# Layout of the inverse DFT's output and of the gated result, between PSUM, VectorE and the last projection

## The chip, the core and the metric

The kernel runs on one core of a Trainium2 chip. The metric is the device time of one execution in microseconds. Inside the core, TensorE multiplies matrices from SBUF into PSUM (PE is the multiplication, PEld the load of the stationary operand, the "weights"), VectorE (DVE) and ScalarE (ACT) work on vectors and read PSUM, GpSimd (POOL) works on SBUF, and SyncE (SP) issues DMA transfers.

## The reference

Two blocks follow each other, on four sequences of 6272 steps with 256 channels, all in float32.

```python
sig = 1 / (1 + exp(-f_logit)); f = lower_bound + (1 - lower_bound) * sig; i = 1 - f
h = f[:, t] * h + i[:, t] * x[:, t]          # for each t; x = all h
proj = x @ w_proj                            # 256 -> 3 * 256: x1, x2, x3
X2 = rfft(x2, axis=1); H = rfft(filter_fft, axis=0)
x2_conv = irfft(X2 * H, n=6272, axis=1)      # a circular convolution over the sequence
out = (x1 * x2_conv * x3) @ w_out
```

## The kernel before

Time is written as 128 x 49: a step t has an index m (128) and a residue r (49). The Fourier transform over 6272 is done as a transform over m, one over r, the product with the filter's transform, and the two inverses, all as matmuls. float16 is used for most operands; the last projection takes float32r, a four-byte matmul type.

The stages for a batch b are these.

- `hgrn(b)`: x and f_logit are loaded in 13 chunks of up to 512 steps (L275), the sigmoid runs on ScalarE (L278), the product on GpSimd (L280), both are turned with channels on the partitions (L287), the recurrence is a scan on VectorE (L304), x1 and x3 are projected (L315) and multiplied into z (L323, L326). z[b] keeps x1 * x3 in float16, channels on the partitions and time along the free axis.
- `wraps`, `phase_p`, `phase_f1`, `mini`: copies of h, the x2 projection (L589), the transform over m (L604).
- `units(b)`: 16 units with the transform over r (L648), the product with the filter (L658) and the inverse over r (L668), whose result is left in Th.
- `phase_o(b)`: the output. It runs over r in twelve groups of four and a last group of one (rn is the size of the group). For each group it does the inverse DFT over m into two banks of PSUM, one for each half p of the channels (L693, two 64-row matmuls for each r and p), the gate: the product with z into the buffer ys (L700), the projection with w_out, in which ys is the stationary operand (L710, two matmuls for each r, 256 columns each), the copy out of PSUM into one of two output buffers (L715, in helper lines L248 on ScalarE and L253 on VectorE), and the store (L719). ys has two buffers, taken in turn; PSUM has eight banks, and L693 and L710 each take two at a time.

In the kernel before, a group's PSUM bank and its ys row hold the time index m outside and the residue i inside: element m * rn + i. Thus L693 writes every rn-th element of the bank, the gate reads and writes one run, and L710's weights `y[:, kh, :, i]` are every rn-th element of the row. z is read as `zr[:, :, :, r0:r0 + rn]`, runs of rn elements with a step of 49 between runs.

The order of the work isn't that of the program text. `op` records each piece with a cost for each engine that may do it, its reads and its writes; `Plan.emit` then issues the pieces by a list scheduler that uses these costs and an estimate of transfer times. So hgrn(b + 1) is interleaved with units(b) and phase_o(b) on every engine, and each engine then carries out its own list in that order. The first `emit` covers the preparation of the filter and hgrn(0), the second all the rest.

The preparation has similar shapes: L519 is a float32r matmul of 256 columns whose weights are contiguous, the copy behind it reads PSUM with the residue innermost, 256 elements apart, in a helper line (L251 on VectorE, into f), and L379 writes weights with a step of four float16 elements.

Of the kernel before, what the change touches and what calls it, by code (L numbers as in the profile page):

```python
# [46 lines left out]
def m0_of(r):  # L47
    return (128 * q_of(r) - r) // Q


class Plan:
# [20 lines left out]
    def op(self, cost, fn, r=(), w=(), kb=0.0, table=None, take=0, src=None):  # L72
        preds = set()
        for t in r:
            if t in self.writer:
                preds.add(self.writer[t])
        for t in w:
            if t in self.writer:
                preds.add(self.writer[t])
            preds.update(self.readers.get(t, ()))  # L80
        me = len(self.ops)
        if src is not None:
            preds.add(src)
            self.ops[src]["users"].append(me)
        self.ops.append(dict(cost=cost, fn=fn, preds=preds, kb=kb, table=table, end=None,
                             eng=None, succ=[], take=take, src=src, users=[], at=None))
        for p in preds:
            self.ops[p]["succ"].append(me)
        for t in r:
            self.readers.setdefault(t, set()).add(me)  # L90
        for t in w:
            self.writer[t] = me
            self.readers[t] = set()
        return me
# [89 lines left out]
def kernel(  # L184
# [10 lines left out]
    nc = tc.nc  # L195
# [36 lines left out]
    PS = psp.tile([128, 8, 512], F32, name="PS")  # L232
# [10 lines left out]
    def copy(e, dst, src, scale=None):  # L243
        if e == "ACT":
            if scale is None:
                nc.scalar.copy(dst, src)  # L246
            else:
                nc.scalar.activation(dst, src, AF.Copy, scale=scale)  # L248
        elif e == "DVE":
            if scale is None:  # L250
                nc.vector.tensor_copy(dst, src)  # L251
            else:
                nc.vector.tensor_scalar(dst, in0=src, scalar1=scale, scalar2=None,  # L253
                                        op0=AOP.mult)
        else:
            nc.gpsimd.tensor_copy(dst, src)

    def either(n, runs=1.0):

        return {"ACT": 0.06 + runs * n / 1200.0, "DVE": 0.08 + runs * n / 960.0}  # L260
# [418 lines left out]
    def phase_o(b):  # L679
        zr = zt[b % 2][:].rearrange("p k (m r) -> p k m r", r=Q)  # L680
        tf = Th[:].rearrange("p c a g -> p (c a g)")
        for g, r0 in enumerate(range(0, Q, 4)):
            rn = min(4, Q - r0)

            def inv(e, cb, r0=r0, rn=rn):
                for i in range(rn):
                    r = r0 + i
                    sh = (128 - m0_of(r)) % 128
                    for rr in range(2):
                        c0 = (rr * Q + r) * 128  # L690
                        for p in range(2):
                            ps = slice(64 * p, 64 * p + 64)
                            nc.tensor.matmul(PS[:, cb + p, i:i + rn * 127 + 1:rn],  # L693
                                             tf[ps, c0:c0 + 128], ID[ps, rr, sh:sh + 128],
                                             start=(rr == 0), stop=(rr == 1))
            i1 = op({"PE": 0.235 * rn}, inv, r=[("Th", u) for u in range(NU)] + ["Th"], take=2)
            yk = g % 2
            y = ys[:, yk, :, 0:rn * 128].rearrange("p a (m i) -> p a m i", i=rn)
            op({"DVE": 0.08 + rn * 0.27}, lambda e, cb, y=y, r0=r0, rn=rn:
               nc.vector.tensor_tensor(  # L700
                   y, PS[:, cb:cb + 2, 0:rn * 128].rearrange("p a (m i) -> p a m i", i=rn),
                   zr[:, :, :, r0:r0 + rn], op=AOP.mult),
               r=[("z", b % 2, jb, c) for jb in range(2) for c in range(NCHK)],
               w=[("y", yk)], src=i1)

            def proj(e, ob, y=y, rn=rn):
                po = PS[:, ob:ob + 2].rearrange("m a (r e) -> m (a r) e", e=256)
                for i in range(rn):
                    for kh in range(2):
                        nc.tensor.matmul(po[:, i, :], y[:, kh, :, i], Wo[:, kh, :],  # L710
                                         start=(kh == 0), stop=(kh == 1))
            po = op({"PE": 0.34 * rn}, proj, r=[("y", yk)], take=2)
            k = count["o"] % 2
            count["o"] += 1
            op(either(256 * rn), lambda e, ob, k=k, rn=rn: copy(  # L715
                e, osb[k][:, 0:rn, :],
                PS[:, ob:ob + 2].rearrange("m a (r e) -> m (a r) e", e=256)[:, 0:rn, :], OS),
               r=[("x2o", i) for i in range(14)] if k else [], w=[("osb", k)], src=po)
            op({"SP": 0.5}, lambda e, k=k, r0=r0, rn=rn: nc.sync.dma_start(  # L719
                out[b].rearrange("(a r) d -> a r d", r=Q)[:, r0:r0 + rn, :],  # L720
                osb[k][:, 0:rn, :]),
               r=[("osb", k)] + ([("x2o", i) for i in range(14)] if k else []), kb=128 * rn)
# [8 lines left out]
    with tc.manual_schedule():  # L731
# [13 lines left out]
        ys = cv.tile([128, 2, 2, 512], F32R, name="ys")  # L745
# [7 lines left out]
        for b in range(B):  # L753
            units(b)
            phase_o(b)
            if b + 1 < B:
                hgrn(b + 1)
                wraps()
                phase_p(b + 1)
                phase_f1(b + 1)  # L760
                mini(b + 1)
# [31 lines left out]
```

## Time and profile before

| What | Value |
|---|---|
| Time, median of 3 runs | 654.3 us (652.3 to 658.98) |
| The profiled execution: time, and the span from its first to its last instruction | 655.55 us, 653.4 us |
| Mean granted TensorE clock in it | 0.953 |
| PE, DVE, ACT, POOL busy | 86%, 78%, 58%, 23% of the span |
| DMA, mean rate | 199 GB/s |

The profile lists busy time by engine, the chain of work that ended last (followed back from the last instruction, at each step to what released it), and groups of instructions: line, engine, operation, output and inputs by name, shape, count, then busy time and mean duration in ns, then the idle time before them with what ended it. A line of a windows view gives a stretch of the span, its length, the busy time of each engine (with the count of instructions), the granted clock, the busy share of the DMA engines and what they moved. A timeline row gives start, duration and count of merged instructions. The row of a single line gives minimum, median and maximum duration. Names are cut by the program: X, for instance, stands for X2, and the second output buffer lies in X2.

### The profile page before, as it was taken

The page shows a single profiled execution, that of the slowest core. Times are in us where ns is not written, and L with a number is a line of the kernel's source. Part 1 is how long each engine was busy: PE and PEld are TensorE (multiplying, and loading weights), DVE is VectorE, ACT ScalarE, POOL GpSimd, SP SyncE. Part 2 cuts the span into 40 slices and gives each one's busy share as a digit, 9 for nine tenths or more (in the row PEclk, how much of TensorE's full clock was granted, in tenths as well). Part 3 has the DMA queues.
Part 4 walks back from the last instruction along what each step waited for, and adds up shares of the span by engine and source line. Part 5 has one row for each costly group of instructions (what it writes and reads, how often), then busy time and mean ns, then how long its engine had stood idle before and what let it go on. Part 6 is the DMA issues. An engine that isn't in the chain of part 4 may idle for free.

```text
span 653.4 us, 12392 instructions
## 1 busy us (share of the span) xinstructions
PE 559.9 (86%) x4821; PEld 430.0 (66%) x4821; DVE 512.2 (78%) x576; ACT 381.2 (58%) x490; POOL 149.8 (23%) x161
## 2 busy tenths in 40 slices
PE   3677888977799999897769999988789999968997
PEld 3455555764478886774538986954568887644786
DVE  7768787589978769699889467899987668999632
ACT  3788786794343558793445456964456567833333
POOL 5424420122104223213222132031023220011000
PEclk9989999899979999998898999999899999997898
DMA  8957755556659786435698588134598862055144
GB/s 310 382 178 256 237 164 172 178 170 192 179 167 333 245 300 211 146 129 180 196 266 266 180 276 282 65 97 148 159 258 293 301 219 108 1 162 160 41 186 170
DMA packets 77643, 130.09 MB, mean 199 GB/s; under 512 B 4878, under 2 KB 56146, under 8 KB 77586
## 3 DMA queue, kind: packets, MB, share of 16 engines
q1 hardware_dynamic: 77586, 129.31, 59.9%
q8 instruction: 38, 0.62, 0.4%
q14 instruction: 19, 0.16, 0.1%
HBM read 84.54 MB, written 32.11 MB: 179 GB/s over the span
## 4 chain that ended last, share of the span: by engine, by line
PE 53%; DVE 14%; DMA 13%; ACT 7%; issue 5%; POOL 2%; SPq 1%; DVEq 0%; ACTq 0%; POOLq 0%
PE PS L710 13%; PE PS L287 10%; PE PS L315 8%; DVE PP L658 8%; PE PS L693 6%; DMA FL<-in_f_logit_dram 6%; PE PS L589 5%; PE PS L668 3%; PE PS L604 2%; PE PS L648 2%; DVE HA L304 2%; ACT X L246 2%; DMA XT<-in_x_dram 2%; DMA H<-HA 2%; DMA Hu<-H 2%
## 5 line engine op out<-in xcount | busy, mean ns | idle before, releaser
L280 POOL TENSOR_TENSOR XT<-XT,FL 128x1024 f32<-128x1024 f32 (+1 forms) x52 | 116.4, 2238 | 266.4 <-DMA XT<-in_x_dram 117.6
L658 DVE TENSOR_TENSOR PP<-PS,Hu 98x1008 f16<-98x1008 f32 x128 | 145.6, 1200 | 8.9 <-PE PS L648 3.0
L246 ACT CAST X<-PS 128x784 f16<-128x784 f32 (+2 forms) x92 | 91.7, 1007 | 84.4 <-PE PS L668 77.2
L304 DVE TENSOR_TENSOR_SCAN HA<-fTs,HA,PS 128x512 f16<-128x512 f32 (+1 forms) x96 | 114.6, 1205 | 29.2 <-PE PS L287 20.7
L315 PE MATMUL PS<-HA,W 128*128 128x512 f16 (+1 forms) x416 | 106.5, 376 | 6.0 <-DVE HA L304 3.9
L299 ACT ACTIVATE fTs<-PS,nomc 128x512 f32<-128x512 f32 (+1 forms) x104 | 69.5, 669 | 65.2 <-PE PS L287 46.1
L710 PE MATMUL PS<-Wo,ys 128*128 128x256 f32 x392 | 102.5, 405 | 0.5 <-DVE ys L700 0.5
L710 PEld LDWEIGHTS PS<-Wo,ys 128*128 128x128 f32 x392 | 94.1, 325 | 5.6 <-issue 3.7
L700 DVE TENSOR_TENSOR ys<-PS,z 128x1024 fp32r<-128x1024 f32 (+1 forms) x52 | 60.6, 1178 | 42.0 <-PE PS L693 37.6
L668 PEld LDWEIGHTS <-PP 98*128 98x128 f16 x1024 | 55.8, 105 | 51.4 <-POOL PP L651 20.9
L668 PE MATMUL PS<-VA,PP 98*128 98x98 f16 x512 | 62.7, 220 | 21.7 <-DVE PP L658 9.9
L323 ACT ACTIVATE x1s<-PS 128x512 f32<-128x512 f32 (+1 forms) x104 | 59.0, 576 | 33.1 <-PE PS L315 23.7
L326 DVE TENSOR_TENSOR z<-PS,x1s 128x512 f16<-128x512 f32 (+1 forms) x104 | 66.4, 651 | 14.9 <-ACT x1s L323 10.4
L287 PE MATMUL PS<-iden,FL 128*128 128x128 f32 x392 | 67.1, 296 | 12.4 <-ACT FL L278 12.4
L287 PE MATMUL PS<-iden,XT 128*128 128x128 f32 x392 | 65.3, 289 | 8.9 <-POOL XT L280 7.3
L278 ACT ACTIVATE FL<-FL 128x1024 f32<-128x1024 f32 (+1 forms) x52 | 52.5, 1010 | 22.2 <-DMA FL<-in_f_logit_dram 22.1
L287 PEld LDWEIGHTS PS<-iden,XT 128*128 128x128 f32 x392 | 48.1, 148 | 25.2 <-POOL XT L280 10.4
L315 PEld LDWEIGHTS <-W 128*128 128x128 f16 x416 | 37.4, 100 | 39.3 <-issue 15.3
L668 PE MATMUL PS<-VB,PP 98*128 98x98 f16 x512 | 62.5, 220 | 0.0
L287 PEld LDWEIGHTS PS<-iden,FL 128*128 128x128 f32 x392 | 49.3, 152 | 19.6 <-ACT FL L278 9.8
L648 PE MATMUL PS<-HA,FT 64*128 64x512 f16 x256 | 41.8, 402 | 20.8 <-ACT X L246 19.2
L693 PE MATMUL PS<-ID,X 64*128 64x128 f16 x784 | 51.3, 309 | 1.0 <-ACT X L248 0.5
(90 smaller groups left out, 583.4 us busy)
## 6 DMA issues: line engine op xcount, KB each, us to landing
Hu<-H SPq DMA_DIRECT2D x64, 392.0 KB
FL<-in_f_logit_dram SPq DMA_DIRECT2D x48, 512.0 KB
XT<-in_x_dram SPq DMA_DIRECT2D x48, 512.0 KB
out_dram<-X SPq DMA_DIRECT2D x24, 512.0 KB
out_dram<-osb SPq DMA_DIRECT2D x24, 512.0 KB
HA<-in_moe_filter_fft_dram SPq DMA_DIRECT2D x12, 512.0 KB
HA<-HA SPq DMA_DIRECT2D x16, 384.0 KB
H<-HA SPq DMA_DIRECT2D x16, 196.0 KB
```

The lines of the kernel that those rows point to most:

```text
L246: nc.scalar.copy(dst, src)
L280: op({"POOL": 0.1 + 0.535 * nb}, lambda e, xt=xt, ft=ft: nc.gpsimd.tensor_tensor(xt, xt, ft, op=AOP.mult), r=[("ft", k)], w=[("xt", k)])
L287: nc.tensor.transpose(PS[:, p, j * 128:(j + 1) * 128], src[:, j, cols], iden[:])
L299: nc.scalar.activation(fT, PS[:, p, 0:n], AF.Identity, scale=nomc[:, kh:kh + 1], bias=1.0),
L304: nc.vector.tensor_tensor_scan(h, fT, PS[:, p, 0:n], init, op0=AOP.mult, op1=AOP.add),
L315: nc.tensor.matmul(PS[:, p, 0:n], W13[:, kh, js], HA[:, HB[kh] + t0:HB[kh] + t0 + n], start=(kh == 0), stop=(kh == 1))
L326: nc.vector.tensor_tensor(zz, PS[:, p, 0:n], xs, op=AOP.mult),
L658: nc.vector.tensor_tensor(PP[:TB, k, o, :, :, 1:64], px.unsqueeze(1).broadcast_to([TB, 2, UE, 63]), hh[:, :, :, 1:64], op=AOP.mult)
L668: nc.tensor.matmul(PS[:, ib + o, pr * TB:(pr + 1) * TB], PP[:TB, k, o, n, 2 * pr:2 * pr + 2, :], v[:TB], start=(n == 0), stop=(n == 1))
L693: nc.tensor.matmul(PS[:, cb + p, i:i + rn * 127 + 1:rn], tf[ps, c0:c0 + 128], ID[ps, rr, sh:sh + 128], start=(rr == 0), stop=(rr == 1))
L700: nc.vector.tensor_tensor(y, PS[:, cb:cb + 2, 0:rn * 128].rearrange("p a (m i) -> p a m i", i=rn), zr[:, :, :, r0:r0 + rn], op=AOP.mult),
L710: nc.tensor.matmul(po[:, i, :], y[:, kh, :, i], Wo[:, kh, :], start=(kh == 0), stop=(kh == 1))
```

## The change

The inverse DFT over m is written as 128 consecutive elements for each r: element i * 128 + m. The gate keeps its order of iteration (m outside, i inside), so it now reads PSUM and writes ys with a step of 128 four-byte elements between neighbours, and reads z as before. `y` keeps its form for the projection, so each L710 load takes 128 consecutive elements of ys. In the group with rn = 1 nothing differs. The costs that the planner is given are not changed.

```diff
@@ phase_o
-                            nc.tensor.matmul(PS[:, cb + p, i:i + rn * 127 + 1:rn],
+                            nc.tensor.matmul(PS[:, cb + p, i * 128:(i + 1) * 128],
                                              tf[ps, c0:c0 + 128], ID[ps, rr, sh:sh + 128],
                                              start=(rr == 0), stop=(rr == 1))
             i1 = op({"PE": 0.235 * rn}, inv, r=[("Th", u) for u in range(NU)] + ["Th"], take=2)
             yk = g % 2
-            y = ys[:, yk, :, 0:rn * 128].rearrange("p a (m i) -> p a m i", i=rn)
+            y = ys[:, yk, :, 0:rn * 128].rearrange("p a (i m) -> p a m i", i=rn)
             op({"DVE": 0.08 + rn * 0.27}, lambda e, cb, y=y, r0=r0, rn=rn:
                nc.vector.tensor_tensor(
-                   y, PS[:, cb:cb + 2, 0:rn * 128].rearrange("p a (m i) -> p a m i", i=rn),
+                   y, PS[:, cb:cb + 2, 0:rn * 128].rearrange("p a (i m) -> p a m i", i=rn),
                    zr[:, :, :, r0:r0 + rn], op=AOP.mult),
```

## The prediction

> **What bounds the kernel now.** I read the page first: busy shares, then the chain that ended last.
>
> ```profile
> span 653.4 us, 12392 instructions
> ...
> PE 559.9 (86%) x4821; PEld 430.0 (66%) x4821; DVE 512.2 (78%) x576; ACT 381.2 (58%) x490; POOL 149.8 (23%) x161
> ...
> PE 53%; DVE 14%; DMA 13%; ACT 7%; issue 5%; POOL 2%; SPq 1%; DVEq 0%; ACTq 0%; POOLq 0%
> PE PS L710 13%; PE PS L287 10%; PE PS L315 8%; DVE PP L658 8%; PE PS L693 6%; DMA FL<-in_f_logit_dram 6%; PE PS L589 5%; PE PS L668 3%; PE PS L604 2%; PE PS L648 2%; DVE HA L304 2%; ACT X L246 2%; DMA XT<-in_x_dram 2%; DMA H<-HA 2%; DMA Hu<-H 2%
> ```
>
> TensorE holds half of the chain; the two lines whose operands change, L693 and L710, hold 19% of the span. But VectorE is 78% busy, and the change gives it work. So I cut the span into stretches: the first four below are the four output phases (the first three with the next batch's recurrence interleaved), the last four the unit phases.
>
> ```profile
> core 0: us, PE busy (x) PEld busy (x) DVE busy (x) ACT busy (x) POOL busy (x), PEclk, DMA share, GB/s
> 186.00:252.00 66.00, 65.13 (x500) 55.19 (x500) 50.35 (x49) 35.05 (x49) 19.25 (x10) 0.98 0.80 268
> 357.00:400.00 43.00, 42.02 (x326) 36.46 (x322) 25.43 (x25) 21.74 (x29) 9.87 (x6) 1.00 0.74 253
> 487.00:542.00 55.00, 53.71 (x414) 45.89 (x413) 36.60 (x37) 34.21 (x47) 17.64 (x10) 1.00 0.79 275
> 610.00:650.00 40.00, 37.65 (x300) 33.25 (x297) 16.50 (x16) 13.01 (x16) 0.00 (x0) 0.99 0.36 145
> 121.00:186.00 65.00, 49.52 (x583) 37.10 (x581) 58.97 (x55) 37.97 (x41) 13.72 (x21) 0.97 0.61 181
> 293.00:357.00 64.00, 48.43 (x477) 35.31 (x478) 56.29 (x52) 28.63 (x38) 18.08 (x22) 0.87 0.74 222
> 431.00:487.00 56.00, 45.72 (x471) 29.09 (x470) 55.01 (x58) 26.24 (x38) 9.78 (x18) 0.97 0.56 165
> 570.00:610.00 40.00, 31.25 (x329) 18.50 (x328) 38.06 (x37) 14.56 (x19) 5.05 (x16) 0.83 0.43 132
> ```
>
> In the first three (A, B, C) PE is full (65.13 of 66, 42.02 of 43, 53.71 of 55) while DVE has 15.7, 17.6 and 18.4 us free. In the unit phases DVE is the full one: together 208.3 of 225 us, 92.6%, which I use below as the share a bounding DVE reaches. The last output phase (D) has nothing beside it; its rhythm:
>
> ```profile
> 611.98 2.36 DVE L700 TENSOR_TENSOR ys<-PS,z 128x1024 fp32r<-128x1024 f32 x2 [0.43 <-PE PS L693]
> ...
> 637.75 1.94 PEld L710 LDWEIGHTS PS<-Wo,ys 128*128 128x128 f32 x8 [0.21 <-issue]
> 637.75 2.14 PE L710 MATMUL PS<-Wo,ys 128*128 128x256 f32 x8
> 637.86 1.23 DVE L700 TENSOR_TENSOR ys<-PS,z 128x1024 fp32r<-128x1024 f32 x1 [1.83 <-PE PS L693]
> ...
> 639.83 1.05 PE L693 MATMUL PS<-ID,X 64*128 64x128 f16 x16
> ...
> 640.80 2.14 PE L710 MATMUL PS<-Wo,ys 128*128 128x256 f32 x8
> ```
>
> One group of four r lasts 3.05 us (637.75 to 640.80), all of it PE; the gate on DVE idles 1.83 us of it.
>
> **The change, part by part.** No number that the planner works with is edited, so the order on every engine and queue should stay, DMA issues included; only durations move. Three do.
>
> ```profile
> L710 PEld LDWEIGHTS PS<-Wo,ys x392: 186/329/335, 191.1 to 648.2; 128*128 128x128 f32 x196
> L710 PE MATMUL PS<-Wo,ys x392: 280/396/514, 191.2 to 648.3; 128*128 128x256 f32 x196
> ...
> 38.10 0.53 PEld L519 LDWEIGHTS PS<-afs,rot 128*128 128x128 f32 x4 [0.92 <-ACT afs L246]
> ...
> 645.93 0.28 PE L693 MATMUL PS<-ID,X 64*128 64x128 f16 x4
> ```
>
> (1) L710's weight load. Eight loads take 1.94 us at 329 ns each: one per (1.94 - 0.33)/7 = 230 ns, and the matmuls keep that pace. The minimum, 186 ns, is the last group of each batch, where rn = 1 and the stride is already one. L519 has the same shape and type with contiguous weights: four in 0.53 us, (0.53 - 0.19)/3 = 114 ns apart. So 230 becomes about 115: 0.92 us less per group of eight.
>
> (2) L693's store to PSUM. Its two 64-row halves run side by side; 16 in 1.05 us at 311 ns each is a pair per (1.05 - 0.31)/7 = 106 ns. The rn = 1 group stores contiguously: two pairs in 0.28 us at about 0.22, so some 0.06 per pair. Saved 8 x 0.04 = 0.32 us. PE's group falls by 1.24 us, from 3.05 to 1.81.
>
> (3) The gate L700. Each of its 1024 elements now comes from PSUM 512 bytes after the one before, within four interleaved runs, and goes to SBUF in the same way. No row shows that write; the nearest:
>
> ```profile
> L326 DVE TENSOR_TENSOR z<-PS,x1s 128x512 f16<-128x512 f32 x96 | 64.5, 681 | 14.0 <-ACT x1s L323 9.5 <-PE PS L315 3.8
> L700 DVE TENSOR_TENSOR ys<-PS,z 128x1024 fp32r<-128x1024 f32 x48 | 57.8, 1218 | 39.2 <-PE PS L693 34.8 <-ACT osb L248 4.3
> ...
> L251 DVE CAST f<-PS 128x512 fp32r<-128x512 f32 x14 | 9.3, 689 | 5.9 <-PE PS L519 4.0 <-ACT f L246 1.9
> ...
> L700 DVE TENSOR_TENSOR ys<-PS,z 128x256 fp32r<-128x256 f32 x4 | 2.8, 696 | 2.9 <-PE PS L693 2.9
> ...
> L379 DVE CAST W<-HA 128x128 f16<-128x128 f32 x4 | 1.2, 305 | 0.0
> ...
> L253 DVE TENSOR_SCALAR osb<-PS 128x256 f32<-128x256 f32 x1 | 0.4, 416 | 0.0
> ...
> L460 DVE CAST D<-tout 128x128 f16<-128x128 f32 x1 | 0.2, 222 | 0.0
> ```
>
> - Read side: the filter's L251 (into f) reads PSUM 1024 bytes apart element by element, and its 689 ns stand beside 681 for a contiguous 512: no cost.
> - L379 writes SBUF one element in every 8 bytes: 305 against L460's 222, 0.65 ns an element.
> - The small L700 (rn = 1) reads z one element in every 98 bytes: 696 against 416 for a contiguous 256, 1.10 ns an element.
>
> The ends are 0 and, if a short-hop and a wide-hop cost add, 1.75 ns an element. The write side is L379's kind, the width of the hop is z's; I take the middle of these two, 0.87 ns. L700 becomes 1.22 + 0.89 = 2.11 us. Nothing gains on DVE.
>
> The Trainium skill speaks against this part: "Vector Engine (DVE) Microarchitecture Reference", section "Measured stream behaviour on trn2", gives a destination that hops at every element 1.71 ns per column for 4 KiB hops and 2.50 for 24-word steps, against 1.054 contiguous. No run here has yet shown either; as an estimate from that page L700 would be 1.9 or 2.7 us, and the sum below 623 or 658 us.
>
> **The sum.** The gate's count per stretch:
>
> ```profile
> 186.00:252.00 66.00, 15.03 (x13) 0.98 0.80 268
> 357.00:400.00 43.00, 12.89 (x11) 1.00 0.74 253
> 487.00:542.00 55.00, 12.59 (x11) 1.00 0.79 275
> ```
>
> One in each is the small one, unchanged; so 12, 10 and 10 grow by 0.89.
> - A: PE 65.1 - 12 x 1.24 = 50.2. DVE 50.35 + 10.7 = 61.0, over 0.926 is 65.9. Gain 0: DVE takes over as the bound where PE leaves it.
> - B: PE 29.6, DVE 34.3, so 37.1: gain 5.9. C: PE 41.3, DVE 45.5, so 49.1: gain 5.9. DMA, busy 0.74 x 43 = 31.8 and 0.79 x 55 = 43.5 us, would stand at 0.86 and 0.89 there; for loads that then come late I take 1 us off each: 5 and 5.
> - D: after L700(g) PE needs 0.95 for L710(g), 0.5 for L693(g+2) and some 0.3 between, 1.8 in all; DVE needs 2.11 - 0.08 (two L700 in a row took 2.36, not 2.44) = 2.03, and ys has two buffers. So DVE is continuous: the first gate starts near 611.7, the twelfth ends near 611.7 + 11 x 2.03 + 2.11 = 636.1. L710 of that group starts there, 10 us earlier than now (row 646.15 below), and takes 0.9 less. Gain 11.
>
> ```profile
> 646.15 2.41 PE L710 MATMUL PS<-Wo,ys 128*128 128x256 f32 x10
> 646.26 0.71 DVE L700 TENSOR_TENSOR ys<-PS,z 128x256 fp32r<-128x256 f32 x1 [1.06 <-PE PS L693]
> 647.14 0.33 SPq L719 DMA_DIRECT2D out_dram<-X  x1
> ...
> 649.86 0.38 ACT L248 ACTIVATE X<-PS 128x256 f32<-128x256 f32 x1 [0.44 <-DMA out_dram<-X]
> ```
>
> The output loop of D is not the limit: a store issued at 647.14 frees its buffer by 649.86, 2.7 us, with 1.02 for the ScalarE copy 3.8 us for two buffers, 1.9 per group.
>
> Sum 0 + 5 + 5 + 11 = 21 us. The profiled execution took 655.55 (span 653.4), 1.25 above the median of 654.3; against the median the forecast is 633 us. Each further 0.1 us on L700 costs (32/0.926 + 12) x 0.1 = 4.7 us, so the sum hangs on (3).
>
> The unit phases, filter and recurrence are left as they are. PE's wait-free cover is gone in A: its clock could fall as in 293 to 357 (0.87 with PE 76% busy), but 50.2/0.87 = 57.7 still lies below DVE's 65.9.
>
> **The rivals.**
> - *Wide writes are nearly free.* For it: L251's row, where four interleaved streams cost nothing. Against: both rows where every element hops alone. Then DVE no longer binds: A at its DMA share of 0.95, 0.80 x 66/0.95 = 55.6; B 33.5; C 45.8; D 1.9 per group, 12.5 saved. Gain 10.4 + 9.5 + 9.2 + 12.5 = 42: 613 us.
> - *The gate becomes the bound everywhere and eats more than TensorE gives* (slower). Place: DVE in A, B, C. Price: both hop costs add, 1.75 x 1024 = 1.79, L700 3.0 us. A 71.8/0.926 = 77.6 (+11.6), B 46.8 (+3.8), C 58.9 (+3.9), D 0: +19, 673 us. It decides from L700 = 2.6 us on (0 = -21 + 47 x 0.45). For it: DVE's spare time is only 16 to 18 us a phase. Against: no single row reaches it. The skill's 2.50 is this case at 2.7 us.
> - *z's price alone, 1.10:* L700 2.34, A +2.9, B -3.4, C -3.4, D -8: 642 us. This lies inside the forecast's case.
> - *L710 does not speed up*, its pace being set by something else than the stride: only 0.32 us a group on PE, D -3.5, B and C -4 each: 643 us. Against it stand 186 ns and L519.
>
> **How the numbers follow.** Measurement tells about 1% (6.5 us) from no change. L700 between 1.8 and 2.4 us, 620 to 646: 0.51, the forecast. Nearly free, 613 to 620: 0.16. L710 not faster: 0.03. L700 from 2.4 to 2.7, 647 to 661, within 1%: 0.13. Above that, 661 to 675: 0.17. Faster 0.51 + 0.16 + 0.03 = 0.70. The range from 615 to 661 leaves out about 0.04 below and 0.16 above.
>
> **What would show it.** After the change: L710 loads near 190 ns at about 115 ns pace; L693 near 220 ns; L700 2.1 us; in the last phase gates back to back at 2.0 us with PE idle between groups, the chain there going through DVE L700; the first output phase as long as now, with DVE over 90% busy; B and C shorter. It is wrong if L700 leaves 1.8 to 2.4 us, if loads of x and f hold up B and C, or if the instruction order moves.

## The result and the profile after

The changed kernel takes 632.45 us (median of 4 runs, 629.8 to 635.61) against 655.6 us for the kernel before, measured beside it; the ratio is 0.9649, 95% interval 0.9579 to 0.9718. The forecast was 633 us. Medians and ratios here and below are of fast executions: each of the last two kernels had one slower execution, 620.91 and 621.51 us, which is left out. The profiled execution took 632.16 us, its span is 630.0 us. From its page, the span, the busy shares and the chain that ended last:

```profile
span 630.0 us, 12392 instructions
...
PE 506.9 (80%) x4821; PEld 371.5 (59%) x4821; DVE 543.7 (86%) x576; ACT 381.4 (61%) x490; POOL 150.1 (24%) x161
...
PE 35%; DVE 21%; DMA 16%; ACT 9%; issue 8%; POOL 2%; SPq 1%; DVEq 0%; ACTq 0%; POOLq 0%
DVE PP L658 8%; PE PS L287 7%; PE PS L589 7%; PE PS L315 6%; DVE ys L700 5%; DMA FL<-in_f_logit_dram 4%; PE PS L710 4%; DVE HA L304 4%; PE PS L668 4%; DMA out_dram<-X 3%; DMA H<-HA 3%; PE PS L648 3%; PE PS L604 3%; ACT X L246 2%; DMA XT<-in_x_dram 2%
```

TensorE's part of the chain fell from 53% to 35% and L710's from 13% to 4%; VectorE's rose from 14% to 21%, and the gate L700, which was on no listed line before, now holds 5%. TensorE lost 53 us of busy time, VectorE gained 31.5. The order of instructions is that of before on every engine. The three operations, from the rows of their lines (minimum, median and maximum in ns) and the groups by shape:

```profile
L693 PE MATMUL PS<-ID,X x784: 213/216/311, 184.2 to 621.3; 64*128 64x128 f16 x196
```

```profile
L710 PEld LDWEIGHTS PS<-Wo,ys x392: 186/189/337, 188.9 to 623.1; 128*128 128x128 f32 x196
L710 PE MATMUL PS<-Wo,ys x392: 278/282/581, 188.9 to 623.2; 128*128 128x256 f32 x196
```

```profile
L700 DVE TENSOR_TENSOR ys<-PS,z 128x1024 fp32r<-128x1024 f32 x48 | 92.8, 1978 | 5.3 <-PE PS L693 4.1 <-ACT osb L248 0.7
```

L693's median went from 311 to 216 ns, the load of L710 from 329 to 189, the gate from 1.22 to 1.98 us. Where the time went is seen by landmarks. The chain in order of time (start, length, what) has the start of `phase_p`, L589, in each batch and the first gate of the last output phase. Before:

```profile
268.82 10.59 PE PS L589 x95
...
407.72 10.49 PE PS L589 x96
...
547.21 10.70 PE PS L589 x98
```

and after:

```profile
262.98 10.59 PE PS L589 x95
...
398.05 10.49 PE PS L589 x96
...
533.01 10.70 PE PS L589 x98
...
596.15 1.93 DVE ys L700
```

Up to the first L589 the run is 5.8 us shorter; the first L693 had already started at 184.2 instead of 186.1, before anything changed, so 3.9 of it belong to output phase A. The next two stretches fall by 3.8 (138.9 to 135.1) and 4.5 (139.5 to 135.0), but each holds a unit phase as well as B or C. The last unit phase, which is untouched, falls by 1.6, and D, from its first gate to the end of the span, from 41.4 to 33.9, so 7.6.

B and C alone are seen from the first L693 to the start of the last L710 of a batch. Before: the stretch from L589 through the unit phase ahead of B, then B, and C:

```profile
core 0: us, PE busy (x) PEld busy (x) DVE busy (x) ACT busy (x) POOL busy (x), PEclk, DMA share, GB/s
268.82:351.02 82.20, 65.79 (x676) 51.71 (x677) 71.52 (x63) 46.53 (x54) 20.91 (x23) 0.90 0.57 170
351.02:400.40 49.38, 48.40 (x385) 42.00 (x386) 30.96 (x31) 25.51 (x34) 11.92 (x6) 1.00 0.78 264
...
481.02:542.06 61.04, 59.75 (x471) 51.34 (x471) 42.64 (x42) 36.15 (x51) 20.01 (x11) 1.00 0.81 273
```

and after:

```profile
262.98:347.09 84.11, 68.88 (x675) 53.18 (x675) 71.70 (x63) 46.49 (x54) 20.98 (x23) 0.84 0.53 165
347.09:390.84 43.75, 34.49 (x385) 27.29 (x386) 38.73 (x30) 25.86 (x34) 11.15 (x6) 1.00 0.85 295
...
471.75:527.87 56.12, 47.16 (x472) 36.11 (x471) 50.19 (x41) 36.22 (x51) 19.60 (x11) 1.00 0.84 293
```

So B gave 5.6 us and C 4.9; the stretch ahead of B, which the change doesn't touch, took 1.9 us longer, at a granted clock of 0.84 instead of 0.90. The four output phases gave 3.9 + 5.6 + 4.9 + 7.6 = 22.0 us, and the rest of the span 1.4, where the change has no part and executions differ by as much.

A and D after:

```profile
184.20:247.00 62.80, 54.32 (x503) 41.98 (x503) 58.14 (x49) 35.44 (x49) 19.28 (x10) 0.94 0.86 287
...
596.15:630.00 33.85, 23.17 (x273) 19.44 (x267) 23.74 (x13) 12.68 (x13) 0.00 (x0) 0.82 0.48 191
```

VectorE is the full engine in A now, 58.14 of 62.8 us, 92.6%, and the fuller one in B and C (89% in both), with the transfers at 0.84 to 0.86.

### The profile page after: what moved, and what is told of

It reads as the page before. It is cut to its first block, busy times and chain, and to the rows that moved or that the text cites. A ratio compares the mean times of both kernels' runs of the same rounds, so it can differ in the third digit from the quotient of the medians.

```text
span 630.0 us, 12392 instructions
## 1 busy us (share of the span) xinstructions
PE 506.9 (80%) x4821; PEld 371.5 (59%) x4821; DVE 543.7 (86%) x576; ACT 381.4 (61%) x490; POOL 150.1 (24%) x161
## 4 chain that ended last, share of the span: by engine, by line
PE 35%; DVE 21%; DMA 16%; ACT 9%; issue 8%; POOL 2%; SPq 1%; DVEq 0%; ACTq 0%; POOLq 0%
DVE PP L658 8%; PE PS L287 7%; PE PS L589 7%; PE PS L315 6%; DVE ys L700 5%; DMA FL<-in_f_logit_dram 4%; PE PS L710 4%; DVE HA L304 4%; PE PS L668 4%; DMA out_dram<-X 3%; DMA H<-HA 3%; PE PS L648 3%; PE PS L604 3%; ACT X L246 2%; DMA XT<-in_x_dram 2%
## 5 line engine op out<-in xcount | busy, mean ns | idle before, releaser
L315 PE MATMUL PS<-HA,W 128*128 128x512 f16 (+1 forms) x416 | 105.2, 372 | 6.0 <-DVE HA L304 3.5
L700 DVE TENSOR_TENSOR ys<-PS,z 128x1024 fp32r<-128x1024 f32 (+1 forms) x52 | 95.4, 1879 | 5.7 <-PE PS L693 4.5
L668 PEld LDWEIGHTS <-PP 98*128 98x128 f16 x1024 | 55.9, 105 | 51.5 <-POOL PP L651 20.9
L326 DVE TENSOR_TENSOR z<-PS,x1s 128x512 f16<-128x512 f32 (+1 forms) x104 | 66.3, 651 | 13.0 <-ACT x1s L323 11.2
L710 PE MATMUL PS<-Wo,ys 128*128 128x256 f32 x392 | 61.8, 302 | 14.8 <-DVE ys L700 14.3
L287 PEld LDWEIGHTS PS<-iden,XT 128*128 128x128 f32 x392 | 48.3, 149 | 33.9 <-POOL XT L280 17.6
L710 PEld LDWEIGHTS PS<-Wo,ys 128*128 128x128 f32 x392 | 52.2, 198 | 23.9 <-DVE ys L700 13.7
L648 PE MATMUL PS<-HA,FT 64*128 64x512 f16 x256 | 44.3, 423 | 20.6 <-ACT X L246 19.2
L651 POOL COPY PP<-zm 98x32 f16<-98x32 f16 x64 | 20.0, 327 | 142.4 <-PE PS L668 101.7
```

Of the source, the lines that this page charges most:

```text
L287: nc.tensor.transpose(PS[:, p, j * 128:(j + 1) * 128], src[:, j, cols], iden[:])
L315: nc.tensor.matmul(PS[:, p, 0:n], W13[:, kh, js], HA[:, HB[kh] + t0:HB[kh] + t0 + n], start=(kh == 0), stop=(kh == 1))
L326: nc.vector.tensor_tensor(zz, PS[:, p, 0:n], xs, op=AOP.mult),
L648: nc.tensor.matmul(PS[:, xb + e2, :], FT[rows, r, :], A[rows, es, r, :], start=(r == 0), stop=(r == 1))
L668: nc.tensor.matmul(PS[:, ib + o, pr * TB:(pr + 1) * TB], PP[:TB, k, o, n, 2 * pr:2 * pr + 2, :], v[:TB], start=(n == 0), stop=(n == 1))
L700: nc.vector.tensor_tensor(y, PS[:, cb:cb + 2, 0:rn * 128].rearrange("p a (i m) -> p a m i", i=rn), zr[:, :, :, r0:r0 + rn], op=AOP.mult),
```

## The experiments

Times are medians in us, ratios to the kernel before on the same chip. The edits are shown against the changed kernel, shortened where a line or a row of dots says so.

**The gate without its hop.**

```diff
-                   y, PS[:, cb:cb + 2, 0:rn * 128].rearrange("p a (i m) -> p a m i", i=rn),
+                   ys[:, g % 2, :, 0:rn * 128].rearrange("p a (m i) -> p a m i", i=rn),
+                   PS[:, cb:cb + 2, 0:rn * 128].rearrange("p a (m i) -> p a m i", i=rn),
...
```

> This kernel has TensorE as in the changed kernel (contiguous store of L693, contiguous weights of L710), but the gate runs over PSUM and ys in flat order, so it has no hop at all; the product then pairs z with the wrong steps, which leaves the output permuted and the time readable. Theory (the gate's price is what caps the gain): L700 back to 1.22 us, VectorE no longer the bound in the output phases, the forecast's case of nearly free writes: 613 us, between 608 and 620. Rival (the gain is capped by output stores and loads, not by the gate): L700 at 1.22 us, but the time stays within 4 us of the changed kernel's 632.

Measured: 616.06, ratio 0.9417 (0.9381 to 0.9453).

```profile
L700 DVE TENSOR_TENSOR ys<-PS,z 128x1024 fp32r<-128x1024 f32 x48 | 57.6, 1216 | 14.0 <-PE PS L693 12.5 <-ACT osb L248 1.4
```

The gate is back at 1216 ns and waits for TensorE again (12.5 us); the contiguous operands are worth 39 us, and the dearer gate takes 16 of them back. The prediction's case of nearly free writes (613) was 3 us too low.

**Only the PSUM half.** ys and L710 as before.

```diff
-            y = ys[:, yk, :, 0:rn * 128].rearrange("p a (i m) -> p a m i", i=rn)
+            y = ys[:, yk, :, 0:rn * 128].rearrange("p a (m i) -> p a m i", i=rn)
```

> Only the PSUM half of the change: L693 stores contiguously, the gate reads PSUM with the 512-byte step, ys and L710's weights stay as before. Theory (the read hop is free, the write hop is what costs): L700 stays at 1.2 us, L693 near 216 ns, L710's loads 329 ns; 0.32 us less per group of TensorE in 48 groups, so up to 15 us less: 640 to 645 us. Rival (the read hop carries part of the 0.76 us that the gate grew by): L700 between 1.5 and 2.0 us, and the time 645 to 655 us.

Measured: 645.22, ratio 0.9865 (0.9812 to 0.9917).

```profile
L700 DVE TENSOR_TENSOR ys<-PS,z 128x1024 fp32r<-128x1024 f32 x48 | 57.6, 1216 | 30.0 <-PE PS L693 28.2 <-ACT osb L248 1.7
```

The gate reads PSUM with the 512-byte step and takes 1216 ns, to the nanosecond what it takes without one: the read hop is free. The medians of L693 and of L710's load are 217 and 330 ns, as expected. The time stands at the slow edge of what was expected for L693 alone, and the rival's time alone would not have refuted it; the row does.

**Only the ys half.** L693 stores with its step, the gate reads PSUM in one run.

```diff
-                            nc.tensor.matmul(PS[:, cb + p, i * 128:(i + 1) * 128],
+                            nc.tensor.matmul(PS[:, cb + p, i:i + rn * 127 + 1:rn],
-                   y, PS[:, cb:cb + 2, 0:rn * 128].rearrange("p a (i m) -> p a m i", i=rn),
+                   y, PS[:, cb:cb + 2, 0:rn * 128].rearrange("p a (m i) -> p a m i", i=rn),
```

> Only the ys half: the gate reads PSUM contiguously and writes ys with the 512-byte step, L710's weights are contiguous, L693 stores with its step as before. Theory (the write hop is the whole price): L700 at 1.98 us as in the changed kernel, L710 loads 189 ns, L693 311 ns; TensorE then needs 2.1 us a group against 2.0 of VectorE, time 634 to 641 us. Rival (read and write hops share the price): L700 clearly under 1.9 us.

Measured: 635.19, ratio 0.97 (0.9659 to 0.9741).

```profile
L700 DVE TENSOR_TENSOR ys<-PS,z 128x1024 fp32r<-128x1024 f32 x48 | 93.8, 1983 | 8.3 <-PE PS L693 6.8 <-ACT osb L248 0.7
```

The whole price, 1983 against 1216 ns, is on the write. This half carries nearly all of the gain; its interval overlaps the changed kernel's, so what the PSUM half adds on top isn't told from nothing.

**Pairs.** ys holds two rows of pairs, so that each write of the gate has a neighbour and L710 takes every second word.

```diff
-            y = ys[:, yk, :, 0:rn * 128].rearrange("p a (i m) -> p a m i", i=rn)
+                y = ys[:, yk].rearrange("p a x -> p (a x)").rearrange(
+                    "p (h a m l) -> p a m h l", h=2, a=2, l=2)
+                src = PS.rearrange("p b (h l m) -> p b m h l", h=2, l=2)
+                zz = zr[:, :, :, r0:r0 + 4].rearrange("p a m (h l) -> p a m h l", l=2)
...
-                        nc.tensor.matmul(po[:, i, :], y[:, kh, :, i], Wo[:, kh, :],
+                        nc.tensor.matmul(po[:, i, :], y[:, kh, :, i // 2, i % 2], Wo[:, kh, :],
```

> As the changed kernel, but ys keeps the four r of a group as two rows of pairs: the gate writes runs of two adjacent four-byte words, and an L710 load takes every second word. PSUM is contiguous as in the change. Theory (the gate pays for each write that has no neighbour, TensorE pays for a load whose words lie 16 bytes apart): L700 falls to 1.2 to 1.35 us, L710's loads stay near 190 ns, and the time comes to that of the flat gate, 613 to 618 us. Rival one (what costs is the jump itself, each half as many): L700 about 1.6 us and 622 to 626 us. Rival two (a load with any step costs): L710's loads between 230 and 329 ns, and 620 to 632 us. The Trainium skill, Vector Engine (DVE) Microarchitecture Reference, section Measured stream behaviour on trn2, says that a stream keeps its full rate in runs of at least two adjacent four-byte words; by that rule it is the first case.

Measured: 618.95, ratio 0.9438 (0.9376 to 0.95). The gate (L708 in this kernel) and the loads (L716):

```profile
L708 DVE TENSOR_TENSOR ys<-PS,z 128x1024 fp32r<-128x1024 f32 x48 | 57.6, 1216 | 15.2 <-PE PS L693 13.8 <-ACT osb L248 1.2
```

```profile
L716 PEld LDWEIGHTS PS<-Wo,ys x392: 186/196/337, 190.0 to 610.9; 128*128 128x128 f32 x196
```

Both rivals fall, and the first case of the expectation holds: the gate pays nothing for pairs, and a load with an 8-byte step takes 196 ns against 189. The time lies 1 us above the range of that case; within the intervals the kernel gets what the flat gate gets.

**The hop moved to z.** PSUM and ys contiguous, z read two bytes at a time with a 98-byte step.

```diff
-            y = ys[:, yk, :, 0:rn * 128].rearrange("p a (i m) -> p a m i", i=rn)
+            y = ys[:, yk, :, 0:rn * 128].rearrange("p a (i m) -> p a i m", i=rn)
...
-                   y, PS[:, cb:cb + 2, 0:rn * 128].rearrange("p a (i m) -> p a m i", i=rn),
-                   zr[:, :, :, r0:r0 + rn], op=AOP.mult),
+                   y, PS[:, cb:cb + 2, 0:rn * 128].rearrange("p a (i m) -> p a i m", i=rn),
+                   zr[:, :, :, r0:r0 + rn].rearrange("p a m i -> p a i m"), op=AOP.mult),
...
-                        nc.tensor.matmul(po[:, i, :], y[:, kh, :, i], Wo[:, kh, :],
+                        nc.tensor.matmul(po[:, i, :], y[:, kh, i, :], Wo[:, kh, :],
```

> As the changed kernel, but the gate goes over i outside and m inside: PSUM and ys are now read and written in one run, and z, two bytes an element, is read with a step of 98 bytes. The small group of the kernel before put 1.10 ns on such an element, so L700 should take 1.22 + 1.12 = 2.34 us against 1.98. Theory of the prediction (beyond L700 = 2 us VectorE binds in all four output phases, 47 us per us of L700): 642 by its own sum, up to 649 counted from the changed kernel's 632. Rival (the slope stays that between the flat gate's 1.22 us and the change's 1.98, (632.45 - 616.06)/0.76 = 21.6 us per us): 640 us.

Measured: 650.59, ratio 0.9933 (0.9903 to 0.9963).

```profile
L700 DVE TENSOR_TENSOR ys<-PS,z 128x1024 fp32r<-128x1024 f32 x48 | 112.3, 2377 | 4.8 <-PE PS L693 4.7
```

The gate takes 2.38 us, 1.13 ns an element over 1216; from the changed kernel's 1.98 us on, the time rises by 18.1 us for 0.40 us, 45 us per us. The prediction had 47, and the rival's slope of 21.6 falls: below 2 us a cheaper gate meets other limits, above it nearly every us counts in full. In the four output phases, from the first L693 to the last L710 of each, VectorE is now busy 62.0 of 65.0, 44.1 of 47.1, 56.1 of 61.3 and 29.5 of 32.0 us, 92% to 95%: it binds in all of them. The time itself lies 1.6 us above the 649 counted from the changed kernel and 8.6 above the 642 of the prediction's own sum, so the slope was right and the level of the sum too low. With TensorE's savings all in place, most of the gain is gone: the slower case that the prediction put at L700 = 2.6 us was near.

**A third output buffer.** In all batches:

```diff
-            k = count["o"] % 2
+            k = count["o"] % 3
...
+               cv.tile([128, 4, 256], F32, name="osb2")]
```

> The changed kernel with a third buffer for the output, in an SBUF tile of its own, so that a ScalarE copy waits for the store before the last but two. The planner sees the buffer, so the order of instructions may move too. Theory (the last phase gave 7.6 us instead of 11 because copies waited for stores): the last phase becomes 2 to 3 us shorter, about 629 to 630 us, and the waits of the ScalarE copies for stores (13 us in all) go. Rival (the gate alone sets the pace there): time unchanged within 2 us.

Measured: 634.07, ratio 0.9696 (0.9621 to 0.9771). By time alone the rival holds, but the planner moved the order:

```profile
L693 PE MATMUL PS<-ID,X x784: 212/216/311, 210.7 to 626.0; 64*128 64x128 f16 x196
```

The first L693 starts at 210.7 us instead of 184.2, so this run doesn't separate the two. The last phase did get shorter, 31.1 us from the first gate (602.08) to the end of the span (633.2). So the buffer was given to the last batch alone, which leaves TensorE's and VectorE's order as in the changed kernel:

```diff
-            k = count["o"] % 2
+            k = count["o"] % (3 if b == B - 1 else 2)
...
+               cv.tile([128, 4, 256], F32, name="osb2")]
```

> The changed kernel with the third output buffer in the last batch alone; the first three batches keep two, so TensorE's and VectorE's instructions stay in the order of the changed kernel. Theory (in the last phase the copies wait for stores): the ScalarE waits for stores there go, and the phase from its first gate to the end is 2 to 3 us shorter than 33.85 us, so 629.5 to 630.5 us. Rival (the gate, 1.95 us a group, sets the pace to the end): no change beyond 1 us.

Measured: 629.21, ratio 0.9627 (0.9594 to 0.9659). The times don't separate it from the changed kernel, the profile does: from its timeline, VectorE's gates in the last phase (span 624.3):

```profile
593.09 3.74 DVE L700 TENSOR_TENSOR ys<-PS,z 128x1024 fp32r<-128x1024 f32 x2
597.89 1.98 DVE L700 TENSOR_TENSOR ys<-PS,z 128x1024 fp32r<-128x1024 f32 x1 [1.06 <-PE PS L693]
600.11 18.27 DVE L700 TENSOR_TENSOR ys<-PS,z 128x1024 fp32r<-128x1024 f32 x10 [0.23 <-PE PS L693]
```

The phase takes 31.2 us instead of 33.85, as expected. The gates end 25.3 us after their start (26.3 in the changed kernel, below), and from there to the end it is 5.9 instead of 7.5 us. So 1.6 us are the buffer. The other us is TensorE's clock: the gates' two waits for L693 are 1.06 and 0.23 us, with a granted clock of 0.51 from 597 to 599 us and 1.00 from 599 on, against 1.38 and 0.99 in the changed kernel, where it is 0.50 from 598 to 604 (below).

**The planner told the new costs.**

```diff
-            i1 = op({"PE": 0.235 * rn}, ...
+            i1 = op({"PE": 0.15 * rn}, ...
-            op({"DVE": 0.08 + rn * 0.27}, ...
+            op({"DVE": 0.08 + rn * 0.46}, ...
-            po = op({"PE": 0.34 * rn}, ...
+            po = op({"PE": 0.25 * rn}, ...
```

> The changed kernel with the planner told what the operations now cost: 0.15 instead of 0.235 us per r for L693, 0.25 instead of 0.34 for L710, 0.46 instead of 0.27 for the gate. Only the order of instructions can move. Theory (the gate's time is the bound in the output phases, and no order removes it): within 5 us of 632. Rival (the order was made for a gate of 1.2 us and leaves VectorE waiting): 615 to 627 us.

Measured: 643.45, ratio 0.9824 (0.9762 to 0.9887): both missed. Truer costs gave an order that is 11 us slower, with the gate unchanged at 1983 ns. Part of it is seen in the profile: the new order leaves 18 instead of 9 of the products L326 to the last unit phase, where VectorE is the full engine already, so this phase, from L589 to the first gate, takes 68.45 us with 64.9 of VectorE's work instead of 63.1 with 59.1. The last output phase is 2.4 us shorter. Another 5.4 us lie between the first two of the L589 landmarks above; what they wait for stays open.

**The faster version: pairs with the third buffer**, in all batches and in the last alone.

> The pairs with the third output buffer. With the gate at 1.22 us and TensorE at 1.8 us a group, the output loop of two buffers, 3.8 us for two groups, is the next limit in the last phase by the prediction's count: 12 groups at 1.8 instead of 1.9 to 2.2 us. Theory: 2 to 5 us less than the pairs' 619, 614 to 617. Rival (the transfers themselves, busy over 0.9 of the time in the output phases, are the limit): no change beyond 2 us.

> The pairs with the third output buffer in the last batch alone. Theory: the last phase, 31.2 us in the pairs' profile, falls to the 26.3 us that it took with three buffers throughout, so 613 to 615 us. Rival (the shorter phase there came from another order of instructions): 617 to 620 us.

Measured: 614.07, ratio 0.9365 (0.93 to 0.9429), and 613.51, ratio 0.9371 (0.9338 to 0.9404). Both are as expected, and both beat the kernel before and the changed one clearly; from each other and from the pairs with two buffers their intervals don't part them. In the profiles the last phase from the first gate to the end is 31.2 us with two buffers (585.62 to 616.8), 26.3 with three throughout (583.22 to 609.5) and 27.8 with three in the last batch (583.59 to 611.4): the expected 26.3 was missed by 1.5. TensorE's clock accounts for it: with three in the last batch the granted clock is 0.51 from 587 to 589 us and the gates wait 1.62 and 1.15 us for L693, with three throughout it is 1.00 from 587 to 589 and the same two waits are 0.75 and 0.50. Between 31.2 and 26.3 the clock at the start of the phase is 1.00 in both, so there the third buffer accounts for the shorter phase: the chain of the pairs' profile goes through output stores for 48% of the time from 580 us on, with three buffers it goes through L716 and L693. The rival of the transfers falls for the last phase. In the first three, where the transfers are busy 0.90, 0.89 and 0.93 of the time in the pairs' profile, it isn't settled.

## Why the prediction was right, point by point

- **What bounds.** TensorE in A to C before, VectorE after: right. The 92.6% that a bounding VectorE was given is what A shows; B and C stand at 89%.
- **L710 and L693.** The pace of 115 ns a load was read from L519, that of some 60 ns a pair from L693's rn = 1 group. In full-clock groups of the changed kernel eight loads take 1.01 us against 1.94 (row 606.35 below), (1.01 - 0.19)/7 = 117 ns apart, so 0.93 saved for 0.92 forecast. Sixteen L693 take 0.62 us against 1.05, (0.62 - 0.22)/7 = 57 ns a pair, so 0.43 saved for 0.32:

```profile
607.50 0.62 PE L693 MATMUL PS<-ID,X 64*128 64x128 f16 x16
```

- **The gate.** 1.98 us for a forecast of 2.11. Price (1978 - 1216)/1024 = 0.74 ns an element, between the 0.65 of the short hop and the 1.10 of z, and nearer the row that writes. The read side is free as L251 said. The Trainium skill's 1.71 ns per column ("Vector Engine (DVE) Microarchitecture Reference", section "Measured stream behaviour on trn2"), which the prediction turned into an estimate of 1.9 us, came closer than my middle. The Trainium skill's 2.50 is for 24-word steps; this step of 128 words doesn't cost that, and the trace's number decides.
- **The sum.** 0 + 5 + 5 + 11 = 21 against 3.9 + 5.6 + 4.9 + 7.6 = 22.0. The parts are less right than the total, and that 633 lies 0.6 us from the measured 632.45 is partly luck: the gate came 0.13 us cheaper than forecast, which by the prediction's own slope of 47 us per us makes its sum 627; D, below, lost most of that again. A was undersized: the cheaper gate explains 12 x 0.13/0.926 = 1.7 us of the 3.9, the rest I can't assign. The windows of B and C began at 357 and 487 us, while their first L693 starts at 351.0 and 481.0, so that two of the twelve gates of each were left out. Over the whole phases, with twelve gates 0.76 us dearer, the sum's rule gives (30.96 + 9.1)/0.926 = 43.3 us for B and (42.64 + 9.1)/0.926 = 55.9 for C, against 43.75 and 56.1 measured: what was taken off for late transfers, 1 us each, is hardly needed. The chain of B after passes through one load of x, as the chain before does just ahead of B; that late loads hold up B isn't shown. After, then before:

```profile
369.65 8.40 DMA XT<-in_x_dram
```

```profile
348.68 6.52 DMA XT<-in_x_dram
```

- **D is the mis-sized term**, 7.6 for 11. The step that failed is "the output loop of D is not the limit", and with it the sign that the chain there would go through the gates. From 605.5 us to the end the chain of the changed kernel goes through copies of one output buffer and their stores:

```profile
606.58 4.45 DMA out_dram<-X
...
612.18 2.62 DMA out_dram<-X
...
615.96 2.63 DMA out_dram<-X
...
619.74 3.24 DMA out_dram<-X
```

From the timeline of the changed kernel, ScalarE's copies of one output buffer, what ended their wait, and VectorE's gates:

```profile
611.13 1.02 ACT L248 ACTIVATE X<-PS 128x1024 f32<-128x1024 f32 x1 [2.46 <-DMA out_dram<-X]
...
614.91 1.02 ACT L248 ACTIVATE X<-PS 128x1024 f32<-128x1024 f32 x1 [1.55 <-DMA out_dram<-X]
...
618.69 1.02 ACT L248 ACTIVATE X<-PS 128x1024 f32<-128x1024 f32 x1 [1.47 <-DMA out_dram<-X]
...
623.09 1.02 ACT L248 ACTIVATE X<-PS 128x1024 f32<-128x1024 f32 x1 [1.86 <-DMA out_dram<-X]
```

```profile
601.26 1.98 DVE L700 TENSOR_TENSOR ys<-PS,z 128x1024 fp32r<-128x1024 f32 x1 [1.38 <-PE PS L693]
604.24 18.22 DVE L700 TENSOR_TENSOR ys<-PS,z 128x1024 fp32r<-128x1024 f32 x10 [0.99 <-PE PS L693]
```

The loop was worked out as 3.8 us for two groups and measures 3.78, 3.78 and 4.40: 1.9 to 2.2 us a group against 1.95 for the gates. So it was no slack but a second limit beside the first, and its lag is paid after the last gate: with the third buffer in the last batch alone that end is 1.6 us shorter, and the chain there goes through the gates (a third of its time from 588 us on). The other part is TensorE's clock at the start of the phase: the waits before the third and the fourth gate, 1.38 and 0.99 us, lie where the granted clock was half (row 600 to 604: 0.50; in the kernel before it was 1.00 from 612 to 622). Together these 2.4 and 1.6 us are more than the 3.4 that are missing; the cheaper gate gave some back.

```profile
600.00:604.00 4.00, 4.00 (x42) 3.33 (x40) 1.98 (x1) 1.76 (x2) 0.00 (x0) 0.50 0.33 131
```

In that row's time eight contiguous loads took 1.78 us, nearly as long as the strided ones before (1.94):

```profile
601.15 1.78 PEld L710 LDWEIGHTS PS<-Wo,ys 128*128 128x128 f32 x8 [0.20 <-issue]
...
606.35 1.01 PEld L710 LDWEIGHTS PS<-Wo,ys 128*128 128x128 f32 x8 [0.53 <-issue]
```

I had asked what a lower clock does in A and not in D, where nothing else hides it.

- **The rivals.** Nearly free writes are not this kernel but the pairs'. "L710 does not speed up" is refuted. Of z's price alone the gate came near, 2.38 us for 2.34, but the time was 650.6 for 642. The slower case needed a gate of 2.6 us; with z's hop at 2.38 the kernel stood 0.7% under before with VectorE at 92% to 95%, so mechanism and place are borne out.

## What to carry to other kernels

A layout between two engines has a price on each side, and odd cases that the kernel already runs can show them, here the last group with one r and the filter's L519 and L251. The paces on TensorE's side were read from them to within 3 ns, VectorE's write only to within 0.13 us a gate. Before moving a stride from the engine that bounds to another, count that engine's free time in each phase, and look for a layout that neither pays for: runs of two words cost VectorE nothing and the weight load 7 ns. A loop that comes out level with the new bound is to be counted as a limit, not as slack. And a total that agrees doesn't vouch for its terms: here a gate priced too high hid a last phase priced too low.

## What the runs showed of the hardware that was not expected

- A VectorE write of four bytes with a 512-byte step costs 0.74 ns an element more, a read of two bytes with a 98-byte step 1.13, runs of two four-byte words nothing (1216 ns each time), and a read of PSUM with a 512-byte step nothing.
- A four-byte weight load of 128 columns takes 189 ns contiguous, 196 with an 8-byte step and 329 with a 16-byte step: the jump is between the last two, not at the first.
- At half the granted clock the contiguous loads come at (1.78 - 0.33)/7 = 207 ns. Strided loads at the same clock are in the run of the PSUM half alone (608.1 to 609.1 us: 0.50), at (1.26 - 0.33)/4 = 232 ns, as at the full clock (230). So there the layout gains some 25 ns a load, against 113 at the full clock:

```profile
608.15 1.26 PEld L710 LDWEIGHTS PS<-Wo,ys 128*128 128x128 f32 x5 [0.20 <-issue]
```
